# A fused attention and feed-forward kernel on one core: order tables replaced, the last product cut into two column halves

## The chip, the cores and the metric

The kernel runs on one core of one Trainium2 chip. The core has a matrix engine (TensorE, PE in the profile, with PEld for its weight loads), a vector engine (VectorE, DVE), a scalar engine (ScalarE, ACT), a general engine (GpSimd, POOL) and a queue that issues most transfers (SyncE, SP). Each runs its own instructions strictly in order and waits on the others by semaphores. The metric is the device time of one execution in microseconds (us). Lower is better.

## The reference

All shapes are fixed, and everything is fp32 but the two weight matrices, which arrive as 64-bit floats and are turned into 32-bit ones on the chip.

```
x: (B=8, H=8, S=512, D=64)    state: (8, 8, Ns=32, 64)
# attention, for each batch and head, scale = 1/8
xread = softmax(scale * x @ state^T) @ state      # 512 rows of a head read the state
sread = softmax(scale * state @ x^T) @ x          # 32 state rows read x
t = concat([xread, sread], rows)                  # (8, 8, 544, 64)
t = t.transpose(0, 2, 1, 3).reshape(4352, 512)    # 544 rows of each batch
# feed-forward: w_in (512, 2048), w_out (2048, 512)
h = t @ w_in
g = where(h > 0, h, exp(min(h, 0)) - 1)           # ELU
out = g @ w_out                                   # (4352, 512)
```

## The kernel before

The work is cut by batch. For each of the eight batches the state and `w_in` are multiplied into one matrix first (`make_m`), so the read of the state and the first feed-forward layer become one product (`ffn1_plain` for batches 0 and 1, `ffn1_chunk` for the others). ELU follows on ACT and DVE, and then the second layer as a Strassen scheme with seven products in place of eight (`Strassen`; for batches 1 to 7 each of the seven is cut by the same scheme once more, in `Second`). The 32 state rows of all batches (256 rows together) are kept to the end and go through both layers in `states()`: `state_chunk` four times, and then one `Strassen` object of 128-column parts, whose four result blocks are written by `quarter`.

Batches 0 and 1 run side by side in `start()`, while the 16 blocks of weights are loaded and converted (`convert`: two instructions on ACT and four on DVE for each block). During batch b the inputs of batch b+1 are fetched: `load_blocks`, `load_x`, `fetch` (a 512 KB block of the converted `w_in`, kept in DRAM) and `move_state`, which turns a softmax result on DVE and then moves it by 16 transfers of 32 KB on SP. `state_read` on PE needs all 16.

The program order is not that of the source. Every operation is first recorded in a `Plan` with a number, and the five `ORDERS` tables say in which order each engine runs the numbers. `Plan.follow` then steps through the tables with prices of its own to choose PSUM banks, and to decide how many fill matmuls to put into PE's gaps. A fill multiplies the identity by itself into a free bank, as two matmul instructions, and its result is never used; fills are made only in the first 40 us of the planner's time. In the planner a transfer costs its issue time, then its bytes at a rate of its kind one after another, then 2.2 us to land; 0.1 us later its reader may start.

Numbers that are spoken of below:

- 0 and 1: the first states (32 KB each, 0 on SP, 1 on ACT's queue); 2 and 3: the halves of the first weight block (512 KB each); 4 to 7: the rows of x of batch 0 (256 KB each; 4 and 6 on SP, 5 and 7 on ACT); 11 to 14: those of batch 1; 8 and 9: states of batch 1.
- PE: 16 turns the first states (needs 0, 1); 19 and 22 turn x (19 needs 4 and 5; 22 needs 6 and 7); 55 is a `make_m`; 25 the scores of batch 0; 73 and 76 turn x of batch 1, 58 its states; 96 is a product of the first layer of batch 1.
- DVE 26 to 93: the softmax chains of batches 0 and 1 among conversions; 193 and 68 are a maximum and an ELU in it. ACT 84, 88, 90: exponentials and the sum's end of batch 1's softmax; 135: an ACT half of a conversion.
- 944 to 959: the 16 transfers of `move_state` for batch 3, 1053 to 1055: fetches, which may start when `make_m` 1034 has read the old block; 1046: the `state_read`. 2264 to 2279 and 2366: the same for batch 7. 558 and 559: the two stores of batch 0, queued by the moves for batch 2 (586 to 601).
- 2758 on: the second layer of the states. Before the change 2767, 2799, 2809 and 2819 are its four stores (blocks (0,0), (1,1), (1,0), (0,1)); after it 2767, 2800, 2810 (the first three whole blocks written) and 2820, 2830 (two halves of the fourth).

SP's table of before ends with `2809 2799 2767 2819`. Store 2809 is the one of block (1,0), which is finished shortly before the last.

Of the kernel before, what the change touches and what calls it, by code (L numbers as in the profile page):

```python
# [24 lines left out]
    "store": (0.44, 200e3),  # L25
# [15 lines left out]
def in_order(text):  # L41

    ops = []
    for part in text.split():
# [7 lines left out]
        "16 19 22 55 25 73 76 58 185 187 61 79 65 114 111 189 69 118 122 199 201 96 126 100 130 141 144 203 155 "  # L52
        "158 162 170 174 166 232 229 214 206 218 210 246 243 289 254 250 266 262 301 292 304 270 274 308 278 258 "
        "441 409 312 320 410 442 411 316 332 422 324 412 423 413 443 450 444 451 424 328 414 452 425 415 445 453 "
        "446 336 426 416 427 366 428 447 429 479 480 490 481 499 482 454 491 483 448 484 492 485 455 486 493 456 "
        "494 527 495 528 496 529 530 497 531 622 540 532 533 541 534 542 543 549 544 550 545 551 457 552 546 553 "
        "547 554 555 570 556 642 627 569 628 572 638 573 618 619 639 620 640 624 644 664 647 684 648 608 661 669 "
        "660 662 670 666 681 682 692 686 693 696 708 705 742 706 680 711 745 744 746 751 766 753 779 758 807 782 "
        "783 781 788 811 810 790 795 816 831 809 818 834 823 835 840 886 833 842 859 847 863 869-872 891 883 892 "
        "884 972 888 899 902 900 882 904 907 898 988 968 908 977 969 978 970 985 974 1006 986 993 994 990 1003 "  # L60
        "1034 1004 984 1008 1022 1011 1002 1012 1030 1018 1019 1072 1020 1031 1024 1043 1046 1044 1075 1049 1076 "
        "1081 1096 1074 1083 1109 1088 1137 1112 1113 1111 1118 1141 1140 1120 1125 1146 1161 1139 1148 1164 1165 "
        "1153 1170 1216 1163 1172 1189 1177 1193 1199 1302 1201 1202 1212 1213 1232 1214 1221 1218 1200 1222 1228 "
        "1237 1238 1229 1299 1230 1300 1234 1304 1318 1307 1308 1314 1323 1315 1352 1316 1324 1298 1333 1320 1336 "
        "1334 1341 1338 1342 1402 1349 1350 1332 1354 1360 1364 1361 1348 1373 1406 1405 1374 1439 1379 1376 1404 "
        "1411 1442 1443 1418 1413 1448 1426 1450 1441 1467 1469 1455 1470 1491 1471 1476 1494 1495 1478 1500 1493 "
        "1483 1502 1523 1546 1507 1519 1530 1562 1531 1542 1532 1551 1543 1552 1544 1529 1559 1548 1560 1558 1648 "
        "1567 1564 1568 1632 1629 1630 1682 1637 1634 1638 1628 1653 1645 1654 1646 1663 1650 1666 1664 1694 1644 "
        "1671 1668 1672 1662 1679 1690 1678 1691 1680 1734 1684 1703 1704 1732 1709 1769 1736 1735 1706 1741 1773 "
        "1772 1743 1748 1778 1756 1780 1771 1797 1785 1800 1801 1821 1806 1799 1824 1808 1825 1830 1823 1813 1832 "  # L70
        "1853 1837 1849 1859 1860 1872 1861 1862 1876 1873 1881 1962 1874 1882 1878 1889 1958 1890 1892 1894 1897 "
        "1888 1898 1967 1959 1968 1960 1978 1975 1964 1976 1996 1980 1983 1984 2024 1993 1974 1994 2001 2012 1998 "
        "1992 2002 2020 2009 2021 2010 2033 2014 2062 2034 2008 2039 2065 2086 2036 2071 2066 2099 2064 2073 2127 "
        "2102 2078 2103 2101 2108 2130 2131 2110 2136 2129 2151 2115 2143 2154 2155 2138 2160 2153 2206 2162 2179 "
        "2167 2183 2189-2192 2211 2203 2212 2204 2222 2219 2208 2220 2202 2224 2227 2292 2228 2218 2289 2297 2290 "
        "2298 2308 2305 2294 2306 2288 2313 2326 2314 2310 2323 2354 2324 2304 2415 2342 2328 2331 2332 2350 2351 "
        "2339 2322 2340 2378 2344 2363 2338 2364 2381 2382 2369 2387 2366 2418 2380 2389 2424 2394 2419 2426 2402 "
        "2417 2439 2441 2431 2442 2463 2443 2448 2466 2467 2450 2472 2455 2465 2474 2512 2491 2545 2479 2528 2493 "
        "2497 2496 2498 2517 2509 2518 2510 2508 2514 2525 2561 2533 2526 2524 2534 2530 2542 2541 2543 2550 2547 "
        "2551 2557 2566 2558 2559 2567 2634 2576 2563 2579 2577 2664 2584 2581 2585 2595 2592 2603 2593 2604 2597 "  # L80
        "2607 2575 2608 2638 2637 2610 2643 2636 2667 2591 2666 2668 2645 2693 2673 2749 2650 2697 2696 2675 2750 "
        "2680 2751 2721 2702 2725 2724 2695 2704 2709 2752 2758 2730 2723 2759 2753 2732 2754 2760 2781 2737 2755 "
        "2782 2756 2783 2761 2770 2762 2771 2763 2784 2772 2785 2773 2786 2774-2776 2787 2777 2764 2788 2790 2765 "
        "2791 2800 2792 2793 2801 2794 2802 2795-2797 2803 2804 2810 2805 2811 2812 2806 2813 2807 2814-2817 "
    ),
    DVE: in_order(
        "44 45 50 46 51 52 47 53 21 17 24 26-28 32 179 178 31 106 35 108 37 59 40 38 41 39 107 184 109 80-82 86 "
        "193 192 68 85 89 136 91 94 92 95 93 138 137 150 139 72 99 151 152 125 121 153 103 226 224 133 198 225 "
        "238 227 165 129 239 240 173 241 284 177 286 285 169 287 209 217 298 342 418 213 296 297 299 253 349-351 "
        "343 257 536 352 344 265 345 373 269 273 371 281 372 221 374 385 386 261 311 715 387 277 378 388 379 380 "  # L90
        "315 392 393 319 394 381 419 323 395 478 327 421 404 406 405 335 407 331 400 433 420 435 437 477 398 476 "
        "367 399 475 401 434 436 719 501 720 431 488 722 500 438 432 516 577 502 517 339 506 489 505 430 537 509 "
        "439 718 440 538 631 511 535 515 581 634 582 539 513 602 580 585 561 578 458 651 716 576 548 583 584 673 "
        "579 565 654 562 566 564 635 568 567 575 636 676 630 563 655 632 721 637 625 626 656 657 677 652 658 645 "
        "653 603 650 674 633 605 659 604 646 678 672 667 668 687 689 717 679 688 690 695 675 522 712 713 749 750 "
        "754 762 757 764 805 765 786 761 787 791 814 815 803 799 794 798 801 857 819 806 802 804 878 827 826 839 "
        "822 843 880 846 830 855 851 856 874 850 875 916 877 858 854 876 879 932 921 896 915 890 881 894 895 917 "
        "905 924 912 931 913 920 897 981 910 983 914 997 980 926 982 975 976 906 928 930 942 943 911 996 991 992 "
        "998-1000 1009 1015 1010 960 1016 962 961 1017 1001 937 1014 1033 1025 1027 1026 1028 1050 1051 963 1079 "
        "1080 1084 1092 1094 1087 1091 1116 1095 1117 1121 1144 1135 1145 1129 1128 1124 1131 1187 1132 1133 1149 "  # L100
        "1208 1152 1157 1169 1136 1156 1173 1134 1160 1176 1181 1185 1186 1204 1210 1180 1245 1184 1188 1205 1209 "
        "1211 1224 1246 1206 1225 1226 1207 1227 1311 1242 1313 1243 1220 1247 1261 1251 1262 1235 1240 1312 1305 "
        "1241 1244 1310 1327 1306 1254 1328 1250 1326 1329 1256 1330 1321 1258 1267 1331 1260 1273 1272 1322 1344 "
        "1236 1339 1290 1345 1340 1346 1347 1355 1357 1356 1291 1292 1358 1363 1380 1293 1409 1410 1414 1381 1422 "
        "1421 1465 1424 1446 1447 1425 1417 1451 1454 1466 1459 1458 1461 1462 1538 1474 1475 1517 1479 1540 1499 "
        "1482 1487 1486 1503 1463 1506 1515 1511 1516 1534 1535 1510 1490 1464 1536 1518 1514 1556 1539 1537 1541 "
        "1576 1554 1572 1555 1557 1575 1581 1592 1591 1550 1570 1573 1565 1641 1574 1571 1657 1642 1635 1640 1636 "
        "1577 1643 1584 1566 1658 1580 1659 1586 1656 1651 1660 1652 1590 1588 1603 1675 1602 1620 1669 1661 1676 "
        "1670 1597 1674 1621 1677 1623 1693 1685-1688 1622 1710 1711 1739 1740 1744 1751 1752 1776 1777 1747 1754 "
        "1755 1781 1784 1847 1789 1788 1791 1795 1804 1792 1805 1796 1809 1794 1868 1793 1870 1829 1812 1833 1817 "  # L110
        "1816 1836 1841 1845 1820 1864 1846 1840 1844 1906 1865 1869 1848 1905 1902 1871 1866 1884 1885 1867 1900 "
# [127 lines left out]
class Plan:  # L239
# [120 lines left out]
    def follow(self, orders, until=0.0):  # L360
# [41 lines left out]
        while len(done) < len(self.ops):  # L402
# [7 lines left out]
            at_op[e] += 1  # L410
            if e == PE:
                t = free_at[PE]
                while at < until and t + 0.5 < at:
                    free = [i for u, i in banks if u <= t]
                    if free:
                        fills.append((t, free[-1], 0))
# [1297 lines left out]
```

## Time and profile before

Three runs: median 699.07 us (697.97 to 700.95).

| | |
|---|---|
| the profiled execution's own time | 698.52 us |
| its span, first to last instruction | 696.7 us |
| PE busy | 683.2 us, 98% |
| DVE busy | 573.6 us, 82% |
| ACT busy | 327.4 us, 47% |
| POOL busy | 108.2 us, 16% |
| mean granted TensorE clock | 0.995 |
| DMA | 78.56 MB, mean 113 GB/s |

PE is at work nearly all the time, so the first question is where it isn't. "Busy" counts a matmul from its start to its modelled end, and matmuls overlap; the distance from start to start is the true pace. In the answers by time below, a row gives the start, the length, the engine, the operation, and in square brackets the idle time just before it and who ended it.

### The profile page before, as it was taken

To read this page: it belongs to the slowest core of one execution; us is meant where nothing else is said; L and a number is where in the kernel's file an instruction comes from. 1 tells how busy PE (TensorE), PEld (TensorE's weight loads), DVE (VectorE), ACT (ScalarE), POOL (GpSimd) and SP (SyncE) were. 2 spreads that over 40 slices of the span, in tenths; PEclk is the share of its full clock that TensorE was granted. 3 is DMA by queue.
4 is the path that set the end of the run, shared out by engine and by line. 5 is a ranking of instruction groups with operands and counts; after the bars stand their busy time and mean duration, and the time that the engine had idled before them with its cause. 6 is when DMAs were issued, how large, how long until landed. Compare 5 with 4: busy or idle time off the path is not lost.

```text
span 696.7 us, 14737 instructions
## 1 busy us (share of the span) xinstructions
PE 683.2 (98%) x5926; PEld 590.9 (85%) x5926; DVE 573.6 (82%) x895; ACT 327.4 (47%) x728; POOL 108.2 (16%) x133
## 2 busy tenths in 40 slices
PE   8999999999999999999999999999999999999995
PEld 7544577889988998899988998799889998999994
DVE  4999999989859983999589996998499967987651
ACT  4899972111267324833375327731482237511530
POOL 0100000110150122203130152112500233000000
PEclk9999999999999999999999999999999999999999
DMA  9858681006571335440473055231825062101300
GB/s 234 264 182 252 202 251 39 0 1 202 172 172 61 107 96 156 99 122 1 131 174 121 1 145 133 80 102 49 229 57 137 1 198 92 62 1 38 115 0 31
DMA packets 111268, 78.56 MB, mean 113 GB/s; under 512 B 89184, under 2 KB 92768, under 8 KB 111200
## 3 DMA queue, kind: packets, MB, share of 16 engines
q1 hardware_dynamic: 108988, 77.06, 39.0%
q8 instruction: 47, 0.77, 0.5%
q10 hardware_dynamic: 2212, 0.56, 0.5%
q14 instruction: 21, 0.17, 0.1%
HBM read 61.34 MB, written 13.11 MB: 107 GB/s over the span
## 4 chain that ended last, share of the span: by engine, by line
PE 84%; DVE 5%; DMA 3%; ACT 2%; SPq 2%; issue 1%; POOL 1%; POOLq 0%; ACTq 0%; DVEq 0%
PE ps L525 84%; SPq L525 2%; DVE sec L525 1%; DMA xe<-in_x_dram 1%; DMA xr<-xr 1%; ACT sec L525 1%; DVE g L525 1%; DVE s L525 1%; DMA w_half<-w_in_mem 1%; DVE m L525 0%; DVE aT L525 0%; DVE xr L525 0%; DVE w_half L525 0%; ACT w_half L525 0%; POOL xr L525 0%
## 5 line engine op out<-in xcount | busy, mean ns | idle before, releaser
L525 ACT COPY ps<-ps 128x128 f32<-128x128 f32 (+2 forms) x169 | 55.0, 333 | 215.3 <-PE ps L525 167.6
L525 PE MATMUL ps<-aT,m 128*128 128x256 f32 (+1 forms) x568 | 150.1, 406 | 0.2
L525 PEld LDWEIGHTS ps<-aT,m 128*128 128x128 f32 x568 | 104.6, 190 | 29.9 <-issue 13.5
L525 PE MATMUL ps<-w_out,g 128*128 128x128 f32 (+1 forms) x768 | 116.5, 293 | 0.0
L525 PEld LDWEIGHTS ps<-w_out,g 128*128 128x128 f32 x768 | 102.1, 192 | 6.2 <-ACT m L525 0.8
L525 DVE TENSOR_TENSOR o<-o,ps 128x256 f32<-128x256 f32 (+1 forms) x106 | 55.8, 540 | 40.9 <-PE ps L525 35.8
L525 POOL TENSOR_TENSOR m<-m 128x256 f32<-128x256 f32 x72 | 56.9, 810 | 113.4 <-ACT m L525 112.5
L525 POOL TENSOR_TENSOR xr<-xr,small 128x512 f32<-128x512 f32 x24 | 28.9, 1216 | 276.6 <-DVE small L525 203.3
L525 PE MATMUL ps<-sec 128*128 128x128 f32 x560 | 71.8, 275 | 0.0
L525 PE MATMUL ps<-t_w,s 128*128 128x128 f32 (+1 forms) x432 | 68.8, 298 | 0.0
L525 PEld LDWEIGHTS ps<-sec 128*128 128x128 f32 x560 | 67.0, 192 | 0.4 <-DVE aT L525 0.4
L525 ACT ACTIVATE xe<-ps 128x512 f32<-128x512 f32 x96 | 56.3, 598 | 16.6 <-PE ps L525 7.9
L525 PEld LDWEIGHTS ps<-t_w,s 128*128 128x128 f32 x432 | 59.2, 192 | 3.5 <-issue 0.8
L525 DVE SCALAR_TENSOR_TENSOR g<-xe,ps 128x512 f32<-128x512 f32 x66 | 43.8, 681 | 8.3 <-ACT xe L525 8.0
L525 ACT COPY m<-ps 128x512 f32<-128x512 f32 (+1 forms) x56 | 28.7, 532 | 30.9 <-PE ps L525 30.9
L525 ACT ACTIVATE xe<-xe 128x512 f32<-128x512 f32 x66 | 41.2, 634 | 1.1
L525 DVE TENSOR_TENSOR ps<-sec,ps 128x512 f32<-128x512 f32 (+1 forms) x52 | 34.7, 669 | 8.2 <-PE ps L525 6.0
L525 PE MATMUL ps<-aT,s 128*128 128x256 f32 x168 | 41.3, 380 | 0.0
L525 ACT COPY sec<-ps 128x512 f32<-128x512 f32 (+1 forms) x52 | 29.5, 568 | 23.0 <-PE ps L525 23.0
L525 PE MATMUL ps<-w_out,sec 128*128 128x256 f32 (+1 forms) x176 | 38.3, 351 | 0.0
L525 PE MATMUL ps<-sec,g 128*128 128x128 f32 (+1 forms) x300 | 37.1, 270 | 1.2 <-DMA g<-in_x_dram 0.7
L525 PEld LDWEIGHTS ps<-sec,g 128*128 128x128 f32 (+1 forms) x300 | 34.0, 185 | 2.1 <-DMA g<-in_x_dram 0.9
(148 smaller groups left out, 1163.0 us busy)
## 6 DMA issues: line engine op xcount, KB each, us to landing
w_half<-w_in_mem SPq DMA_DIRECT2D x54, 512.0 KB, 4.3
t_w<-in_moe_w_out_dram SPq DMA_DIRECT2D x8, 1024.0 KB, 5.2
t_w<-in_moe_w_in_dram SPq DMA_DIRECT2D x7, 1024.0 KB
out_dram<-o SPq DMA_DIRECT2D x14, 512.0 KB, 2.8
xe<-in_x_dram SPq DMA_DIRECT2D x26, 256.0 KB, 3.7
o<-in_x_dram SPq DMA_DIRECT2D x80, 64.0 KB, 2.6
w_in_mem<-w_half SPq DMA_DIRECT2D x8, 512.0 KB, 4.0
xr<-xr SPq DMA_DIRECT2D x96, 32.0 KB, 2.6
```

The lines of the kernel that those rows point to most:

```text
L525: ins = getattr(engine, name)(**named)
```

## The change

1. `DMA_COST` gets a price for the four state stores, `store_q`: 0.44 us to issue and 90 GB/s. Before, they had the default of 370 GB/s. The price exists only in the planner.
2. All five `ORDERS` tables are replaced. Most numbers move by a few places.
3. The rule for fills: a fill is put in while the gap has more than 0.35 us left (before 0.5), one every 0.25 us (before 0.3).
4. In `states()`, block (1,0) is now the last one. Its first product (y, already in a bank) is added on DVE at once; its last product, `a22` by `t_w[4]`, is computed in two halves of 128 columns in banks of their own, and each half is added on DVE and stored on its own, as 64 KB. Before, block (0,1) was last: one product of 256 columns, a copy on ACT, one store of 128 KB.
5. The `between` argument of `Strassen.product`, which no call used, goes, and the price of a step becomes an argument.

```
-    "store": (0.44, 200e3),
+    "store": (0.44, 200e3), "store_q": (0.44, 90e3),
...
 PE  (first numbers)
-16 19 22 55 25 73 76 58 185 187 61 79 65 114 111 189 69 118 122 199 201 96
+16 19 22 55 25 73 58 76 187 185 61 79 65 111 114 189 69 122 118 201 199 96
 PE  (last numbers)
-2790 2765 2791 2800 2792 2793 2801 2794 2802 2795-2797 2803 2804 2810 2805 2811 2812 2806 2813 2807 2814-2817
+2765 2791 2787 2792 2788 2793-2798 2811-2813 2801-2808 2814 2821 2815 2822 2816 2823 2817 2824 2818 2825-2828
 DVE (27 us on)
-82 86 193 192 68 85 89 136 91 94 92 95 93
+82 86 192 68 193 85 89 136 91 94 92 95 93
 ACT (23 us on)
-186 57 183 64 188 134 63 66 116 135 112 117 67 113 84 190 194 88 191 195 90
+188 57 63 64 135 186 134 66 116 67 112 190 191 84 113 88 70 117 194 90 148 196 195
 SP  (first numbers)
-2-4 0 6 10-12 9 14 13 8 15
+2 3 0 4 6 10 12 11 13 8 14 9 15
 SP  (moves for batch 2)
-558 525 586 293 593 589 606 590 588 592 594 607 595 600 523 559 597 599 616 601 596 615 587 598 591 617
+558 606 598 594 586 559 588 587 593 592 600 596 617 601 590 526 597 615 524 591 616 589 595 599 523
 SP  (moves for batch 3)
-938 868 959 952 950 951 954 939 957 946 1053 958 955 1054 1055 956 949 947 945 948 953 944 1029
+938 1055 957 953 941 954 947 1053 955 958 952 956 1054 948 946 950 939 945 949 959 940 944 951 1029
 SP  (moves for batch 7)
-2275 2266 2268 2272 2269 2277 2374 2271 2265 2276 2373 2261 2278 2279 2267 2375 2274 2270 2264 2273 2349
+2269 2268 2275 2274 2267 2278 2277 2265 2266 2276 2264 2373 2279 2272 2273 2271 2270 2374 2375
 SP  (last numbers)
-2659 2613 2809 2799 2767 2819
+2659 2602 2613 2767 2800 2810 2820 2830
...
-                while at < until and t + 0.5 < at:
+                while at < until and t + 0.35 < at:
...
-                    t += 0.3
+                    t += 0.25
...
-        quarter(o, 0, 0)
+        piece(o, 0, 0, 0, 2)
...
         o.copy(y, 1, 1)
+        o.plus(y, 1, 0)
         o.product(x1, o.s, t_w[1], False)
         o.plus(x1, 1, 1)
-        quarter(o, 1, 1)
-        o.product(y, o.a22, t_w[4], False)
-        o.plus(y, 1, 0)
-        quarter(o, 1, 0)
+        piece(o, 1, 1, 0, 2)
         o.product(x1, o.a12, b22, False)
         o.copy(x1, 0, 1)
-        quarter(o, 0, 1)
+        piece(o, 0, 1, 0, 2)
+        for n in range(2):
+            cols = slice(n * P, (n + 1) * P)
+            y = o.open()[:, :, :P]
+            o.product(y, o.a22, [w[:, :, cols] for w in t_w[4]], True, 0.224)
+            part = o.part(1, 0)[:, :, cols]
+            V.tensor_tensor(out=part, in0=part, in1=y, op=ALU.add)
+            piece(o, 1, 0, n, n + 1)
+
+    def piece(o, c, q, first, last):
+        cols = slice(q * DM // 2 + first * P, q * DM // 2 + last * P)
+        rows = slice(c * P // NS, (c + 1) * P // NS)
+        dma(out_b[rows, S:SB, cols], o.o_sb[c][:, 0, cols], kind="store_q")
```

## The prediction

> **What bounds the kernel now.** I read the page's busy rows first, then the busy time by stage, which says where PE isn't at work.
>
> ```profile
> PE 683.2 (98%) x5926; PEld 590.9 (85%) x5926; DVE 573.6 (82%) x895; ACT 327.4 (47%) x728; POOL 108.2 (16%) x133
> ...
> 10.30:14.50 4.20, 3.24 (x69) 1.70 (x67) 1.54 (x4) 1.39 (x3) 0.00 (x0) 1.00 1.14 323
> 14.50:21.50 7.00, 5.70 (x70) 4.79 (x63) 6.76 (x11) 5.82 (x14) 2.05 (x2) 1.00 0.94 185
> 21.50:36.50 15.00, 14.28 (x160) 7.45 (x160) 13.63 (x25) 13.43 (x33) 2.06 (x2) 0.89 0.72 255
> 64.00:680.00 616.00, 614.64 (x5275) 548.25 (x5275) 520.26 (x814) 275.64 (x625) 103.33 (x122) 1.00 0.37 103
> 689.10:696.70 7.60, 0.00 (x0) 0.00 (x0) 0.00 (x0) 0.37 (x1) 0.00 (x0) 0.81 0.22 69
> ```
>
> Columns: length, then busy time of PE, PEld, DVE, ACT, POOL, then clock, DMA share, GB/s. From 64 to 680 us PE lacks 1.36 us of 616: reordering can win no more than that there, but it can lose. Time to be had lies at both ends: 7.6 us after the last matmul, and a start in which DVE, not PE, is full (6.76 of 7.00, 13.63 of 15.00). The timelines of the tail, then its DMA by microsecond:
>
> ```profile
> 687.19 1.89 PE L525 MATMUL ps<-w_out,g 128*128 128x256 f32 x8
> 687.39 0.75 DVE L525 TENSOR_TENSOR o<-o,ps 128x256 f32<-128x256 f32 x2 [3.41 <-PE ps L525]
> 687.84 2.56 SPq L525 DMA_DIRECT2D out_dram<-o  x4
> 689.12 0.37 ACT L525 COPY o<-ps 128x256 f32<-128x256 f32 x1 [10.42 <-PE ps L525]
> ```
> ```profile
> 689.00:690.00 1.00, 0.08 (x1) 0.00 (x0) 0.00 (x0) 0.37 (x1) 0.00 (x0) 1.00 0.22 47
> 692.00:693.00 1.00, 0.00 (x0) 0.00 (x0) 0.00 (x0) 0.00 (x0) 0.00 (x0) 1.00 0.27 87
> 695.00:696.00 1.00, 0.00 (x0) 0.00 (x0) 0.00 (x0) 0.00 (x0) 0.00 (x0) 0.50 0.07 24
> ```
>
> All four stores are issued from 687.84 on, because 2809 stands first in SP's table and waits for the addition at 687.39; block (0,0), added at 683.56 by DVE's rows, and block (1,1) wait behind it. The four then share one slow path: 0.52 MB at some 91 GB/s, 0.27 of the 16 DMA engines, until about 695.25. That share is 4.3 engines, and the new stores have the same four rows outermost, so I keep 91 GB/s. The Trainium skill ("DMA: Bandwidth & Descriptors", Rules for kernel authors) has it so: an outermost dimension of fewer than 16 confines a transfer to so many engines.
>
> The stalls in mid-kernel and the start, both from PE's timeline:
>
> ```profile
> 266.19 1.37 PE L525 MATMUL ps<-xe,xr 128*32 128x64 f32 x64 [0.85 <-DMA xr<-xr]
> ```
> ```profile
> 572.01 1.43 PE L525 MATMUL ps<-xe,xr 128*32 128x64 f32 x64 [0.39 <-DMA xr<-xr]
> ```
> ```profile
> 10.35 0.28 PE L525 MATMUL ps<-sec,g 64*128 64x64 f32 x2
> 10.46 0.66 PE L525 MATMUL ps<-sec,xe 64*128 64x64 f32 x16
> 11.77 0.79 PE L525 MATMUL ps<-sec,xe 64*128 64x64 f32 x16 [0.65 <-DMA xe<-in_x_dram]
> 13.46 1.09 PE L525 MATMUL ps<-o,kT 64*32 64x512 f32 x16 [0.31 <-DVE o L525]
> 14.49 2.27 PE L1672 MATMUL ps<-sec 128*128 128x128 f32 x18
> ```
> ```profile
> 30.76 0.69 DVE L525 SCALAR_TENSOR_TENSOR sec<-sec,ps 128x512 f32<-128x512 f32 x1 [1.11 <-ACT sec L525]
> ```
>
> Two `state_read`s (1046 and 2366) wait for `move_state`: 1.24 us, nearly all that PE lacks there. Line 1672 is the fills.
>
> **The change part by part.** The sum is made against the profiled execution: span 696.74, own time 698.52, so 1.78 lie outside; the median, 699.07, is 0.55 above it.
>
> *The end.* Pace first: eight 128x256 instructions run 1.89 us of which the last takes 0.38, so 0.216 each; 24 of 128x128 (2.84 us at 656.21, the last 0.275) give 0.112. A product is 8 steps of two instructions: whole 16 x 0.216 = 3.45, in halves 32 x 0.112 = 3.57. Cost +0.12. Let E be the end of the last matmul (689.09 before; the span ends at E+7.65). After: the 128-column addition, from the 256- and 512-column rows (0.414 and 0.685, thus 0.14 + 1.06 per thousand) 0.28; with 0.03 before and after it SP issues at E+0.34. Before, the first issue at 687.84 had its data flowing at 689.1, 1.27 later: E+1.61. Data: 64 KB at 91 GB/s is 0.72. Last byte to end of span was 696.74 - 695.25 = 1.45. So E+3.8. Are earlier stores out of the way? By PE's new table 13 half-width steps (2 x 0.112 each, 2.9 us) follow block (0,1): copied and issued by E-2.5, its 1.44 us of data done by E+0.2. The first half has 4 steps (0.9) behind it: issued at E-0.56, data from E+0.7 to E+1.4. Free. The unknown is a packet of 512 bytes, half as long as before. If its cost is all bytes, E+3.8; if all per packet, each half takes 1.44, they queue, and the last ends at E+0.7+2.9+1.45 = E+5.05. I take the middle, E+4.4, since no store row is of this size. Gain 3.25 (2.6 to 3.85). The new addition of y (0.41) falls where DVE idles 3.41 us. The Trainium skill ("DMA: Bandwidth & Descriptors", Rules for kernel authors) speaks against halving: below 64 KB a transfer is mostly overhead. By that the upper end, E+5.05, would hold, and the gain be 2.6.
>
> *Moves and fetches on SP.* For batch 3 the new table puts fetch 1055 ahead of the moves. It waits for `make_m` 1034 (PE's rows: 250.24 to 251.77), and 16 moves queue behind it that used to start at 249.24, so they start 2.5 us later. From 251.8, 16 issues of 0.62 (5 in 3.10), two more fetches (0.53 each) and three loads (0.4 to 1.76) end near 264 to 266; the last move took 2.97 to land: 267 to 269. But 1046 stands five places later on PE, products of 0.89 each, so at some 270: the stall goes, with 1 to 3 us to spare. For batch 7 two of three fetches and a load go elsewhere, and the last move is issued near 567.5 in place of 569.5: that stall goes too. For batch 2, store 559 (issued at 167.94, now after seven fewer moves) holds 13 moves; from 167.9, 13 x 0.62 with five loads and fetches end near 182, landed by 185, and `state_read` ran at 187.56. Gain 1.24 (0 to 1.4).
>
> *All other reordering.* PE's work is unchanged, and it is full already, so there is nothing to win. New waits are possible: products that move forward a place or two stand 0.4 to 0.9 us closer to what they need. Bounds 0 (the order stays as dense as before) and 3 (about as many stalls as the start has now: 1.30 + 0.96 + 0.72 of PE idle in the three early stages). I take 0.3, near the row of 64 to 680, which shows what such an order costs PE beside those two stalls: 0.12.
>
> *Fills and the first loads.* The planner decides the number. Its prices put 1, 2, 3, 5, 4, 7, 0 on the wire in this order before, so 0 lands at 10.97 and 16 can start at 11.07: (11.07-0.5-0.7)/0.3 gives 33 fills, and the trace has 66 instructions. With 0 ahead of 4 and the new rule: 16 at 9.12, again 33 fills, (9.12-0.35-0.7)/0.25; but then 4 lands last, 19 can start at 11.07, and 6 fills go between 16 and 19, one more between 19 and 22. On the chip the 33 end as before (the first run slow, then 0.22 each), so 16 stays at 10.35. Six fills, 1.34 us, and some 0.2 to change over put 19 at 11.9, and 22 at 12.75, not 11.77: x has long landed, and PE is busy with work nobody uses. What waits: the copy, scores 25 (at 14.4), then DVE's softmax chain that starts at 14.71, all 0.98 later. In the next gap the 9 fills become 11 or 12, which delays 73 too, but ACT reaches its copy late. DVE runs without a pause from 14.71 to 29.65, so +0.98 arrives there in full; then it idles 1.11 waiting for ACT (row above) and some 0.25 in three pieces up to 36.45, where PE's 96 waits for it. ACT's table now does 135 in a hole (0.73 and 0.79 us idle before PE's products at 24.59 and 27.54) and 84 and 88 earlier. If ACT keeps up, all is absorbed and 0.4 won; if not, 0.98 is lost. I take -0.2 (-0.4 to +1.0). The clock stood at 0.86, 0.50 and 0.79 in the stages 20-22, 22-24 and 24-26. The skill ("TensorE: Matmul & The Clock Gate", Why this matters for your kernels) blames idle gaps over 3 us; here the longest was under 1, after sparse work, so the measurement goes beyond it. By its rule denser fills do nothing here; by the rows they could lift 3.4 us of half clock, 1.7 of PE time, but DVE is full at 2.00 of 2 there: nothing.
>
> Sum: +0.12 - 3.25 - 1.24 + 0.3 - 0.2 = -4.27, so 694.3 for the profiled one, 694.8 for the median.
>
> **The rivals.** About 0.5%, 3.5 us, is what a measurement of this kernel can tell from no change.
>
> *Tail alone*: stores overlap, the order is merely another one. Stalls like today's (0), tail at its poorer end, -2.6 + 0.12 + 0.3 - 0.2: 696.7. For it: 512-byte packets. Against: moves of batch 7 end 2 us sooner.
>
> *Fills eat it*: the start loses 0.98, the packet cost is in the middle, and stalls stay: -3.25 + 0.12 + 0.98 + 0.3 = -1.85, 697.2. For it: DVE has no pause for 15 us. Against: 1.36 us of pauses behind that.
>
> *Slower*: the blocked queue. Fetches and stores stand among the moves in five of six batches, and each `state_read` waits. With the end gaining 3.1, it decides from 0.6 us per batch on (5 x 0.6); at 1.5 us each it costs 7.5 and gives 703.4. For it: 2.5 us of later start in batch 3. Against: `state_read` stands later there, and batch 7's queue is shorter.
>
> *Not what it says*: the early blocks are not stored early. SP's table has 2767 and 2800 first, and by PE's new table 18 whole steps (0.43) and 16 half ones (0.22) follow the first block, 8 and 16 the second: 11.3 and 7.0 us before E. This could only fail through a wait on store 2613; then the tail stays at E+7.65 and the time is 698.1.
>
> **How the numbers follow.** Forecast 0.58 (its own range 692.8 to 695.6); tail alone 0.17; fills 0.14; slower 0.07; not what it says 0.04. The best ends (-3.85 - 1.4 - 0.4 + 0.12 = -5.5) give 693.5, and 0.7 for the spread of runs 692.8. Upward the range takes in tail alone and fills: 698.4, which leaves out slower and a rest. Faster by over 0.5% means under 695.6: the forecast and a little, 0.60; within, 0.33; slower 0.07.
>
> **What the changed profile would show.** Stores of the states at four separate times, the first some 10 us before the last matmul; span end near E+4.4. No `state_read` with an idle time for `xr`. Some 114 to 120 fill instructions (94 before), twelve of them between 10.4 and 11.9, the second x turn near 12.75, yet PE's 96 at 36.0 to 36.6. PE short of about 0.5 us from 64 to 680. I am wrong if E comes later than 689.2, if a stall over 1 us stands before a `make_m` or a `state_read`, or if the halves' data end later than E+3.6.

## The result: 691.8 us, faster than the range

The changed kernel takes 691.79 us (median of 4 runs, 691.65 to 692.47); the kernel before, beside it, 698.52 us (4 runs, 697.14 to 700.95). The ratio is 0.9902, 95% interval 0.9873 to 0.9931. The forecast was 694.8 us with 692.8 to 698.4 around it: right in its sign, too slow by 3 us, and the time lies below the low end. Timed side by side twice more, the same two kernels gave 692.23 and 697.51 us (ratio 0.9922) and 691.79 and 697.43 us (0.9921): a gain of 5.3 to 5.6 us rather than 6.7, with the time after below 692.8 all the same.

The profiled execution has an own time of 691.69 us and a span of 689.9. The busy rows of the page and the busy time by stage, columns as in the prediction:

```profile
PE 683.8 (99%) x5968; PEld 593.6 (86%) x5968; DVE 571.6 (83%) x897; ACT 328.5 (48%) x728; POOL 107.9 (16%) x133
```
```profile
10.30:14.50 4.20, 4.20 (x68) 3.34 (x66) 1.16 (x3) 1.17 (x3) 0.00 (x0) 1.00 1.15 323
14.50:21.50 7.00, 6.56 (x78) 5.18 (x70) 5.57 (x10) 4.47 (x9) 2.06 (x2) 1.00 0.99 256
21.50:36.50 15.00, 14.63 (x181) 7.57 (x181) 14.97 (x27) 14.88 (x38) 2.05 (x2) 1.00 0.65 213
64.00:680.00 616.00, 616.00 (x5308) 550.70 (x5306) 518.77 (x817) 276.88 (x624) 103.08 (x122) 1.00 0.36 102
686.10:689.90 3.80, 0.00 (x0) 0.00 (x0) 0.29 (x1) 0.00 (x0) 0.00 (x0) 1.00 0.15 44
```

Four things are to be seen. From 64 to 680 us PE is now listed as busy in all of 616.00. In the first three stages together PE has 327 instructions, before 299; nearly all of the difference are fills. The clock is 1.00 from 21.5 to 36.5, where it was 0.89. And after the last matmul 3.80 us are left, where there were 7.60. The tail itself, from the timeline:

```profile
683.22 0.37 ACT L525 COPY o<-ps 128x256 f32<-128x256 f32 x1 [6.45 <-PE ps L525]
685.23 0.29 DVE L525 TENSOR_TENSOR o<-o,ps 128x128 f32<-128x128 f32 x1 [5.82 <-PE ps L525]
686.12 0.29 DVE L525 TENSOR_TENSOR o<-o,ps 128x128 f32<-128x128 f32 x1 [0.60 <-PE ps L525]
```

The copy is that of block (0,1); the two additions are the halves of block (1,0), 0.89 us apart. Each half's store was issued at the end of its addition, 685.54 and 686.44, and had landed, by its semaphore, at 687.97 and 688.92: 2.43 and 2.48 us for 64 KB. The 128 KB store of block (0,1), issued at 683.62, had landed at 686.88: 3.26 us.

The two `state_read`s that waited before, in PE's timeline:

```profile
270.05 1.10 PE L525 MATMUL ps<-xe,xr 128*32 128x64 f32 x64
...
569.25 1.10 PE L525 MATMUL ps<-xe,xr 128*32 128x64 f32 x64
```

No bracket stands behind them, so nothing was waited for, and each is 1.10 us long, where the lists of before had 1.37 and 1.43.

To compare the kernels below, a profile is cut in three: the **front**, up to PE's product 96; the **middle**, from there to the end of the last matmul, E; and the **tail**, from E to the end of the span.

| | front | middle | tail | span |
|---|---|---|---|---|
| before | 36.51 | 652.57 | 7.66 | 696.74 |
| after | 36.43 | 649.65 | 3.81 | 689.89 |
| difference | -0.08 | -2.92 | -3.85 | -6.85 |

Of the middle's difference, the two halves of the last product cost 0.12 (32 matmuls at 0.111 us in place of 16 at 0.216, as predicted), so the orders gained 3.04 there.

### The profile page after: what moved, and what is told of

Its sections match the earlier page's. It is cut to its first block, busy times and chain, and to the rows that moved or that the text cites. A ratio compares the mean times of both kernels' runs of the same rounds, so it can differ in the third digit from the quotient of the medians.

```text
span 689.9 us, 14828 instructions
## 1 busy us (share of the span) xinstructions
PE 683.8 (99%) x5968; PEld 593.6 (86%) x5968; DVE 571.6 (83%) x897; ACT 328.5 (48%) x728; POOL 107.9 (16%) x133
## 4 chain that ended last, share of the span: by engine, by line
PE 96%; DVE 1%; ACT 1%; POOL 0%; issue 0%; POOLq 0%
PE ps L525 94%; PE ps L1675 2%; DVE sec L525 1%; ACT sec L525 0%; ACT o L525 0%; ACT w_half L525 0%; POOL sec L525 0%; ACT t_w L525 0%; ACT xr L525 0%; DVE s L525 0%; DVE w_half L525 0%; ACT g L525 0%; POOL sec masks.py:199 0%; DVE o L525 0%; ACT m L525 0%
## 5 line engine op out<-in xcount | busy, mean ns | idle before, releaser
L525 DVE TENSOR_TENSOR o<-o,ps 128x256 f32<-128x256 f32 (+2 forms) x108 | 56.7, 533 | 38.1 <-PE ps L525 29.7
L525 DVE TENSOR_TENSOR ps<-sec,ps 128x512 f32<-128x512 f32 (+1 forms) x52 | 34.8, 671 | 11.0 <-PE ps L525 7.1
L525 PEld LDWEIGHTS ps<-aT,s 128*128 128x128 f32 x168 | 31.9, 190 | 4.3
```

What stands on the lines that cost most here:

```text
L525: ins = getattr(engine, name)(**named)
```

## The experiments

The theory was that tail and middle add up and are separate things, the tail from stores that no longer queue behind block (1,0), the middle from the two `state_read`s. The rivals: that the fills and the clock carry the front and more; that only some of the tail is the halving; that the middle is something else.

### The parts by themselves

`orders_only` has the five new tables up to the second layer of the states and nothing else of the change; `tail_only` the states' new code, price and last places in the tables; `fills_only` the new rule of the fills; `after_old_fills` all but that rule.

```
 orders_only: kernel before, tables up to operation 2757 from after
 tail_only:   kernel before, states() and tables from 2758 on from after
 fills_only:  kernel before
-    while at < until and t + 0.5 < at:      t += 0.3
+    while at < until and t + 0.35 < at:     t += 0.25
 after_old_fills: kernel after, these two lines as before
```

> The kernel before with all five new order tables up to the second layer of the states; the states' code, their order and the rule for fills are the old ones. Theory (orders win 2 us between 36.5 and 689 us, the rest is the tail and the fills bring nothing): the last matmul ends near 686.3, 2.8 us earlier than before, the tail stays at 7.6, span 693.9. Rival (the denser fills and the clock bring the middle's gain too): last matmul at 688 or later, span 695.5 or more.

> The kernel before with the new code and order of the states' second layer alone: column halves, early stores. Theory: the last matmul at 689.2 (0.12 later), the end 3.8 after it, span 693.0. Rival (the stores are early only because the rest of the order is new): the end 5 or more after the last matmul, span 694.5 or more.

> The kernel before with the new rule for fills alone (a margin of 0.35, one every 0.25). Theory (fills are no gain; they hold up the turns of x): 39 or 40 fills before the first turn in place of 33, so the first product that depends on the softmax (96) starts 0.5 to 1.5 us later than 36.5, span 697.2 to 698.2. Rival (fills hold the clock up, which saves up to 1.7 us of PE time): 96 at 35 to 36, span 695.2 to 696.2.

> The changed kernel with the old rule for fills. Theory (fills cost or do nothing): 96 at 35.5 to 36.4, span 689.0 to 689.9. Rival (clock): the half-clock stretch near 21 us returns and 96 starts a microsecond or more later, span 691 or more.

| | time | ratio to before, 95% | front | middle | tail |
|---|---|---|---|---|---|
| before (19 runs) | 698.05 | | | | |
| orders_only | 694.56 | 0.9962 [0.9947, 0.9976] | 34.85 | 649.77 | 7.69 |
| tail_only | 694.74 | 0.9964 [0.9948, 0.9979] | 35.65 | 654.37 | 4.31 |
| fills_only | 697.96 | 1.0001 [0.9988, 1.0014] | 36.78 | 651.32 | 7.79 |
| after_old_fills | 690.97 | 0.9907 [0.9893, 0.9922] | 35.74 | 649.85 | 3.86 |

The orders and the tail are worth 3.5 and 3.3 us, and together (`after_old_fills`) 7.1: they add up. The fills win nothing. In `tail_only`, whose middle is as it was, the wait is still there, by PE's timeline:

```profile
266.78 1.37 PE L525 MATMUL ps<-xe,xr 128*32 128x64 f32 x64 [0.81 <-DMA xr<-xr]
```

This profile's own time, 696.12 us, lies above the median of its ten runs. Most of what its middle is longer than that of before (654.37 to 652.57) comes early: the 0.86 us that it was ahead at 96 were 0.64 us behind by 72 us. At 63.11 PE had waited 1.23 us for a copy on ACT, and that stood behind a conversion that waited for a transfer of weights and started at 60.61 (before at 59.92). So a lead at 96 need not last, and front and middle are best read together.

The tail of `tail_only` is 4.31, not the expected 3.8. Its last store landed 2.89 us after E, as in after (2.84); the rest passed between that landing and the end of the span, 1.43 us against 0.97, for which no run shows the cause.

### What of the tail is the halving

`stores_in_turn` gives the kernel before its stores in the order in which the blocks are done; `last_whole` is the kernel after with the last product in one piece, stored as 128 KB.

```
 stores_in_turn: kernel before
 DVE -2780 2798 2808 2766        +2780 2766 2798 2808
 SP  -2809 2799 2767 2819        +2767 2799 2809 2819
 last_whole: kernel after
-for n in range(2):  (two halves, each added and stored)
+y = o.open()
+o.product(y, o.a22, t_w[4], True)
+o.plus(y, 1, 0)
+piece(o, 1, 0, 0, 2)
```

> The kernel before; only the addition of block (0,0) moves up on DVE, ahead of 2780, 2798 and 2808, and SP takes the four stores as their blocks get ready (2767, 2799, 2809, 2819). No halves. Theory (the tail's gain is mostly that three stores are out of the way): the end 4.6 after the last matmul in place of 7.65, so 3.0 of the 3.85 come from the turn of the stores. Rival (halving gives it): the end stays 6.5 or more after the last matmul.

> The changed kernel with its last product in one piece: one product of 256 columns, one addition, one store of 128 KB; all else as changed. Theory (a packet of 512 bytes costs half of one of 1 KB): last matmul 0.12 earlier, the end 4.6 to 4.7 after it in place of 3.8, so the time rises by 0.7. Rival (packets cost the same, so halving is for nothing): the time falls by 0.1.

`stores_in_turn` took 693.19 us (one run, whose middle was also short, as told below; before 698.10, 7 runs), its tail 4.95. `last_whole` took 693.48 us (692.98 to 693.57; ratio 0.9933, 0.9918 to 0.9947), its tail 4.77. The end of `last_whole` in the timeline:

```profile
684.63 2.32 PE L525 MATMUL ps<-t_w,g 128*128 128x256 f32 x10
685.23 2.75 SPq L525 DMA_DIRECT2D out_dram<-o  x2
686.99 0.42 DVE L525 TENSOR_TENSOR o<-o,ps 128x256 f32<-128x256 f32 x1 [6.49 <-PE ps L525]
```

Here the addition takes 0.42 in place of 0.29, and the store that follows it, the second of the two issues that the SPq row holds, is of 128 KB. So some 2.8 of the tail's 3.85 us are the order of the stores, for which one number moved on DVE and the new order on SP suffice, and 0.96 (4.77 less 3.81) the halving, less its 0.12 on PE. Counted to the landing of the last store alone, the three stand at 6.63 (before), 3.70 (`stores_in_turn`; `last_whole` 3.73) and 2.84 us (after) behind E: 2.9 and 0.9.

### Fills and the clock

In the profile before, the clock was at half from 21.4 to 24.8 us; in after it was not. `first_fills` is the kernel after with fills in the first 9.5 us of the planner's time alone: the long run ahead of 16, and none later.

```
-    steps, fills = plan.follow(ORDERS, 40.0)
+    steps, fills = plan.follow(ORDERS, 9.5)
```

> The changed kernel with fills made only in the first 9.5 us of the planner's time (33, all ahead of the first turn). Theory (the later fills only hold up the turns of x): the second turn of x near 11.8, 96 at 34.8 to 35.5, 0.9 to 1.6 earlier than in the changed kernel, span 688.3 to 689.0. Rival (without them the clock falls to half between 15 and 25 us): a stretch of half clock of 3 us or more, 96 no earlier than 36.4.

It took 692.31 us (691.14 to 693.21; ratio 0.9919, 0.9898 to 0.9940). The clock's dip came back, and twice as long, by the busy time of that stretch:

```profile
18.40:25.20 6.80, 5.38 (x50) 3.55 (x58) 6.80 (x13) 5.73 (x18) 0.20 (x1) 0.50 0.90 316
```

Yet product 96 started at 35.96, earlier than in after: DVE is full in that stretch (6.80 of 6.80). So the dip costs less than the later fills do. That it costs nothing is not shown. The second turn of x, 22, ran at 11.71, as the theory had it, but 96 missed the theory's 34.8 to 35.5: from 22 to 96 it took 24.25 us, in after 23.04 and in `after_old_fills` 23.22, both without a dip. No run separates the half clock from other causes of that microsecond. What the fills cost shows when the other profiles with the new tables are laid side by side. With the new rule 96 starts at 36.43, 37.67, 36.46, 36.84, 36.48 and 37.51; with the old rule at 34.85, 35.74 and 35.58. The means are 36.90 and 35.39. The times say the same, in two pairs.

> The changed kernel as it is, once more, beside the next one: 691.5 to 692.0. Theory and rival agree.

> The changed kernel with the old rule for fills, timed against before on the same chip as the one ahead of it. Theory (the new rule costs 0.5 to 1 us): 690.7 to 691.3. Rival (the first look at it was luck): 691.5 or more.

Beside each other `after_again` (the kernel after, unchanged) took 692.23 us (692.09 to 692.97, 6 runs; ratio 0.9922, 0.9905 to 0.9939) and `after_old_fills_2` 690.64 (689.97 to 690.87, 5 runs; 0.9894, 0.9873 to 0.9914; before 697.51, 23 runs). The kernel after with the old rule for fills beats both kernels, and the new rule costs it some 1.6 us here; by the first `after_old_fills`, against the 691.79 of after, which was not timed beside it, 0.8. PE's timeline of after has the reason, as predicted but for what becomes of it (L1675 is the fills):

```profile
10.79 1.60 PE L1675 MATMUL ps<-sec 128*128 128x128 f32 x12
12.33 0.71 PE L525 MATMUL ps<-sec,xe 64*128 64x64 f32 x16
12.97 0.49 PE L1675 MATMUL ps<-sec 128*128 128x128 f32 x2
13.39 0.71 PE L525 MATMUL ps<-sec,xe 64*128 64x64 f32 x16
...
36.43 4.13 PE L525 MATMUL ps<-s,g 128*128 128x512 f32 x9
```

Twelve fill instructions stand ahead of 19, two ahead of 22, and 22 ran at 13.39 in place of 11.77 before. The old rule in the new tables (`after_old_fills`) has ten ahead of 19 and none ahead of 22, but also 54 ahead of 16 where the new one has 66; there 22 ran at 12.52.

### What the middle gained by

The first test moved the two `state_read`s alone, on PE, in the kernel before.

```
 PE  -1043 1046 1044 1075 1049 1076 1081 1096 1074
     +1043 1044 1075 1049 1076 1081 1096 1046 1074
 PE  -2387 2366 2418 2380 2389 2424    +2387 2418 2380 2389 2366 2424
```

> The kernel before with two places changed on PE: state reads 1046 and 2366 stand six and three operations later (1046 behind the make_m 1096, 2366 behind 2389). Theory (PE waited there for the moves, before the reads and within them): both waits vanish, and the span from product 96 to the last matmul falls by 1.5 to 2.1, from 652.6 to some 650.7. Rival (the gain of the middle is spread over the new order, and these waits would come back elsewhere): it falls by less than 0.8.

It was slower: 701.05 us (700.06 to 701.16), ratio 1.0039 (1.0024 to 1.0054), middle 656.39. PE's timeline says why:

```profile
267.09 1.10 PE L525 MATMUL ps<-aT,m 128*128 128x256 f32 x4 [0.89 <-ACT ps L525]
...
272.20 1.10 PE L525 MATMUL ps<-xe,xr 128*32 128x64 f32 x64
...
274.42 3.72 PE L525 MATMUL ps<-aT,m 128*128 128x256 f32 x16 [1.12 <-ACT kT L525]
```

The read no longer waits. But ACT's table still has its operations in the old order, and one that takes what the read makes now holds ACT up, by ACT's timeline:

```profile
273.37 0.31 ACT L525 ACTIVATE kT<-ps,small 128x64 f32<-128x64 f32 x1 [4.50 <-PE ps L525]
```

PE's products behind the read wait for ACT in turn (1.12 us at 274.42), as do the first ones ahead of it (0.89 at 267.09). So PE's wait for the moves became two waits for ACT, and dearer.

The second left PE as it was and gave SP its moves ahead of the fetches, for batches 3 and 7, with one load of x ahead of each (`moves_first`), and the same with the new tail (`tail_moves`).

```
 SP  -959 952 950 951 954 939 957 946 1053 958 955 1054 1055 956 949 947 945 948 953 944
     +939 959 952 950 951 954 957 946 958 955 956 949 947 945 948 953 944 1053 1054 1055
 (likewise 2261, then 2264 to 2279, then 2374 2373 2375)
```

> The kernel before with one thing changed on SP: for batches 3 and 7 the load of x goes ahead of the 16 moves and the three fetches behind them (before, they stand among the moves). Theory (the two state reads wait for the last move, and how long varies from run to run): no wait before or within 1046 and 2366, the middle from 96 to the last matmul 650.5 to 651.2 in place of 652.6, the median 1 to 2 us under that of before, and the spread of the runs below 1.5 us in place of 2 to 3. Rival (the reads wait for their place in the order, or other waits take over, as when they were moved on PE): the middle stays above 652 and the median within 0.7 us.

> The kernel before with the new second layer of the states and the moves first on SP, nothing else. Theory (the two make nearly the whole gain): the end 3.85 after the last matmul and no waits at the two reads, median 692.0 to 693.5. Rival (the rest of the new tables makes another 1.5 us or more): median 694 or more.

`moves_first`: 696.85 us (695.97 to 698.21, 12 runs; ratio 0.9992, 0.9981 to 1.0002). `tail_moves`: 693.59 (692.93 to 696.03, 10 runs; 0.9948, 0.9935 to 0.9962). Neither has a wait at a `state_read` in its profile, and yet the middles are 651.96 and 652.60. PE's timeline of `moves_first`, and a line of its chain of work that ended last:

```profile
351.05 0.66 PE L525 MATMUL ps<-w_half,kT 64*32 64x256 f32 x16
352.64 1.10 PE L525 MATMUL ps<-w_half,kT 64*32 64x256 f32 x32 [0.93 <-DMA w_half<-w_in_mem]
```
```profile
345.25 7.35 DMA w_half<-w_in_mem
```

The 1.76 us that this profile was ahead of before at 265 us were 0.31 at 359: `make_m` of batch 4 now came early enough to wait for its fetch, which SP's table has behind the moves and among the loads of x. In after the same `make_m` runs from 351.14 without a wait.

So `fetch_early` moves the three fetches of batch 4 up as well, and `after_moves_late` takes from the kernel after just its two stretches of SP's table.

```
 fetch_early: moves_first
 SP  -1285 1383 1395 1384 1401 1394 1385 1396
     +1285 1383 1384 1385 1395 1401 1394 1396
 after_moves_late: kernel after, moves and fetches of batches 3 and 7 in the order of before
```

> The kernel before with the moves of batches 3 and 7 ahead of their fetches (moves_first), and now also the three fetches of batch 4 (1383 to 1385) ahead of its loads of x on SP, directly behind its moves. Theory: after the state_read's wait the next limit was that late fetch, which stood before make_m of batch 4 with 0.93 us. Then make_m has no wait, the lead won at the state_read (some 1.5 us) stays past 360 us, and from PE's 96 to its last matmul it takes 650.6 to 651.4 (moves_first 651.96); time 695.0 to 696.2. Rival, that yet another wait close behind takes it: 651.7 or more, time 696.6 or more.

> The kernel after, with moves and fetches of batches 3 and 7 on SP in the order of before, and nothing else undone. Theory: those two stretches of SP's table carry most of what the middle gained: state_read waits again (some 0.4 to 1 us for batch 3, where it stands a place or two later on PE, and 0.3 to 0.6 for batch 7), from 96 to the last matmul 650.8 to 651.6 (after 649.65), time 693.0 to 693.9. Rival, that the later places on PE alone are enough or that the waits are made good again: within 0.4 us of the kernel after in the same call.

> The kernel after once more, beside the two others: 691.7 to 692.4, from 96 to the last matmul 649.5 to 649.9, no wait before a state_read. It is the measure for after_moves_late.

`fetch_early` took 696.46 us (695.47 to 698.15, 12 runs; ratio 0.9986, 0.9974 to 0.9998; before 697.43, 17 runs). In PE's timeline the wait is gone:

```profile
344.89 6.31 PE L525 MATMUL ps<-aT,m 128*128 128x256 f32 x28
351.13 1.53 PE L525 MATMUL ps<-w_half,kT 64*32 64x256 f32 x48
```

Its middle is 650.79, as the theory had it, and its time 1.0 us better than before, just above what the theory gave. The size has to be taken from the medians, not from that one profile: `stores_in_turn`, with the middle tables of before untouched, happened to have no wait at 264.47 and a middle of 650.57. The old orders have these waits in some executions and not in others.

`after_moves_late` went to the rival in the middle: 692.47 us (692.02 to 693.26; ratio 0.9927, 0.9909 to 0.9944) beside 691.79 (691.52 to 693.37; 0.9921, 0.9901 to 0.9941) of `after_third`, the kernel after, with middles of 649.70 and 649.68. Its median is 0.7 us above, where the rival had at most 0.4, but the ranges overlap and its profile has the difference in front (36.84) and tail (4.24). No read waits, though its last two moves of batch 3 are issued some 3 us later than before the change, by SP's timeline:

```profile
264.31 2.12 SPq L525 DMA_DIRECT2D xr<-xr  x2
```

So SP's order among moves and fetches, which the prediction worked through, is not what lifted the wait in the kernel after. What is left is the read's place on PE. The last run undoes that, for batch 3 alone:

```
 PE  -1043 1024 1044 1018 1049 1075 1076 1096 1046 1081
     +1043 1024 1046 1044 1018 1049 1075 1076 1096 1081
```

> The kernel after with one number moved on PE alone: state_read 1046 is back ahead of 1044, 1018, 1049, 1075, 1076 and 1096, near its place before the change; SP's, DVE's and ACT's tables stay as they are after. Theory: it is this place, with other work of some 5 us put ahead of the read, that took away the wait of batch 3. The last move is issued at 265.36 in the kernel after and took 2.97 us to land in the kernel before, so a read due at 264.99 waits until about 268.3: 3.3 us, of which what stood behind it cannot use any; from 96 to the last matmul 651.9 to 653.0 (after 649.65), time 693.9 to 695.2. Rival, that the slack behind it makes the wait good, or that the moves land sooner: within 0.5 us of the kernel after, 691.4 to 692.6.

One number moved by six places takes away most of what the change won: 696.89 us (695.12 to 697.52, 12 runs), ratio 0.9981 (0.9969 to 0.9993; before 698.06, 17 runs), where after had 0.9902 to 0.9922. The profile's own time, 697.41 us, lies above that median; its middle is 655.29. PE's timeline, then the stretch that follows by the busy time:

```profile
267.75 2.28 PE L525 MATMUL ps<-xe,xr 128*32 128x64 f32 x64 [2.33 <-DMA xr<-xr]
269.96 1.75 PE L525 MATMUL ps<-w_out,g 128*128 128x128 f32 x8
```
```profile
265.43:267.75 2.32, 0.00 (x1) 0.00 (x1) 1.95 (x4) 0.00 (x0) 1.21 (x2) 1.00 0.59 141
267.75:271.20 3.45, 3.45 (x70) 3.25 (x71) 0.00 (x0) 0.00 (x0) 0.00 (x0) 0.51 0.39 157
271.20:274.00 2.80, 2.80 (x24) 2.73 (x24) 0.41 (x1) 0.74 (x2) 0.00 (x0) 0.99 0.00 0
```

The wait is 2.33 us, in place of the expected 3.3, but it isn't all: the clock then stands at half for 3.41 us, in which PE is "busy" throughout and does half the work. The same read takes 2.28 instead of 1.10. Wait and half clock are 2.5 + 1.7 = 4.2 of the 5.6 by which the middle grew over that of after; about 1.1 more was lost between 56 and 70 us, far ahead of the edit, and I have no cause for that.

## Why the prediction was wrong, step by step

By the two profiles, the sum was to be -4.27 and came to -6.85.

**The end** (predicted +0.12 and -3.25, measured +0.12 and -3.85). The mechanism was right: stores at separate times (five of them, not four), a last store of 64 KB, nothing in its way. The term that was off is the price of a 512-byte packet, taken in the middle (E+4.4) between all bytes (E+3.8) and all packets (E+5.05): it is nearly all bytes, 29 ns against 54 for one of 1 KB, and the end came at E+3.81. That this is the low bound to the hundredth is in part luck: the data of the last half took 0.89 us and not 0.72, and from its last byte to the end of the span it was 1.30 and not 1.45. The rule of the Trainium skill that the prediction held against halving ("DMA: Bandwidth & Descriptors", Rules for kernel authors) is of transfers under 64 KB, which the halves are not, and the trace agrees with it as far as it goes: only 0.89 of the last half's 2.48 us were data. It does not lead to E+5.05. One fact in the working was also wrong. Block (0,0) was not added at 683.56; that was block (1,1), and (0,0) stood last on DVE, so SP's order alone would not have freed its store. `stores_in_turn` therefore has an edit in DVE's table too.

**The two `state_read`s** (predicted -1.24). They were worth about 2.2 in the profiles, because the listed idle time is not what is lost. The idle time of 0.85 is counted from the modelled end of the matmul before, 0.275 after its start, while the next could have started at the pace of 0.112: 0.85 + 0.16 = 1.01. Likewise 0.39 + 0.16 = 0.55. And the reads of before were 1.37 and 1.43 long, against 1.10 for one that doesn't wait, 0.27 and 0.33 more. Together 2.16. Of the reasons given for it, one held. For batch 3 the prediction had the later place on PE, and `after_read_early` shows that this is the step that carries it. It had "1 to 3 us to spare", which is right: the last move, issued at 265.36, had landed at 267.25, and the read ran at 270.05. But it laid the later start of the moves to fetch 1055 on SP. In `after_moves_late` no fetch stands ahead of them and they start at 251.86 all the same (after 251.40, before 249.24), right behind DVE's second turn of the state, which ends at 251.70 there and ended at 249.08 before; that points to DVE's table. For batch 7 it had the fetches that go elsewhere, and `after_moves_late` shows that the read doesn't wait even with them back.

**All other reordering** (predicted +0.3, measured about -0.9: 3.04 less 2.16). Here is the step that failed: "From 64 to 680 us PE lacks 1.36 us of 616: reordering can win no more than that there", and from it "it is full already, so there is nothing to win". The row is right and the conclusion isn't. Busy runs to the modelled end, so a pause of less than 0.16 us between two 128x128 matmuls is not seen at all, a longer one is counted 0.16 too small, and pauses inside a group count as work. Adding up the distances from start to start beyond pace (0.112, 0.216 and 0.429 for 128, 256 and 512 columns) over the matmuls on full 128x128 weights from product 96 to E gives 8.16 us for before and 5.71 for after; the 0.60 inside the two reads comes on top. Those 8.8, and not 1.36, are the bound to take there, and the orders won 3.04 of them. By the same token "full" in the new row doesn't mean that nothing is left. Four more waits of over 0.15, 0.76 in all, are gone in after; which places in which table removed each of them was not tried singly, so their cause stays open. Both profiles are single ones, and the old tables' middle varies; but in `stores_in_turn`, where no read waited, it was still 650.57, against 649.53 for after without its 0.12, so about 1 us of this kind is there beside the reads. What the runs do show is that none of the single moves tried makes the gain: the reads alone on PE lose 0.4%, the moves alone on SP change nothing measurable, the moves and a fetch gain 0.14%, all tables 0.38% (the front's share included), the fills' rule left as it was.

**The fills and the first loads** (predicted -0.2, measured -0.08). Near the right size, for the wrong reason. The number was right, 120 instructions (114 to 120 predicted), and so were their places and what they hold up; the delay was larger, 1.62 us for 22 (13.39) where 0.98 (12.75) was forecast. That it would be absorbed was wrong: with the same tables, 96 starts about 1.5 us later under the new rule than under the old one, and that is about the cost of the sixteen instructions by which the old rule has fewer up to 22 (0.112 each, 1.8). What hid this from the comparison is that the new order of the front is better than credited: 35.39, against a mean of 36.05 (35.32 to 37.05) over the seven profiles with old tables and the old rule there. "0.98 lost if ACT doesn't keep up" was nearer. That the clock's dip doesn't matter stays open (`first_fills`, above).

**The rivals.** *Slower*, through fetches among the moves, did not come, and its mechanism is real: `moves_first` met it at batch 4, and `after_read_early` shows its price, some 5 us, at one read. What counts is how far behind the last move the read stands: late moves alone did no harm (`after_moves_late`). *Tail alone* and *Fills eat it* each held one true thing, but the middle won more than they allowed. The range's low end was made from a sum of best cases in which the middle could give no more than 1.4, and that bound was the failed reading above.

## What to carry to other kernels

Where matmuls overlap, bound what a new order can win by the distances from start to start against the pace, not by busy time; a row that says 616.00 of 616.00 can still hide microseconds, though how much of after's 5.71 could be won is not known. Test an order change as a whole: PE's, ACT's, DVE's and SP's places around one wait depend on one another, and one of them moved alone passes the wait on or makes it dearer. And ask of every fill matmul what stands behind it on PE: one put in by a planner's estimate can delay the product that a full DVE is waiting for.

## What the runs showed that was not expected

- Behind a single wait of 2.33 us the granted clock stood at half for 3.41 us, which cost some 1.7 us on top of the wait (`after_read_early`), while the waits of 0.85 and 0.39 us in the kernel before left it at 1.00. The Trainium skill ("TensorE: Matmul & The Clock Gate", What's actually happening) has a window of 3413 ns that runs freely; the half-clock stretches of these runs, 3.41 us here and in before and 6.83 in `first_fills`, fit one window and two. Its rule against idle gaps over 3 us (the same page, Why this matters for your kernels) is too mild for this trace.
- The kernel before spreads by 3.3 us over the 19 runs beside `orders_only` (696.17 to 699.50), `orders_only` by 0.8 over four, and the kernel after by 0.8, 0.9 and 1.9 over four, six and six. In profiles of the old middle tables the read of batch 3 waited 0.85, 0.81, 0.48 and 0.00 us; in the nine of the new ones (`after_read_early` aside, `after_moves_late` with its two stretches of SP's table counted in) none waited, and their middles lie within 0.6 us, from 649.44 to 650.07. The better order looks to be the steadier one too, by fewer runs.
- A 64 KB store of 512-byte pieces with four rows outermost took 2.43 and 2.48 us from issue to landing, a 128 KB one of 1 KB pieces 3.26: the difference is what 64 KB take at some 80 GB/s (the busy time by microsecond has 61, 71 and 45 GB/s there, shared by the three stores). Both have the same number of pieces, so the bytes and not the pieces make the difference.
